# A SwiGLU feed-forward kernel: two weight slabs load behind two blocks of x, and two F tiles of the next tokens run by halves first

## The chip, the core and the metric

The kernel runs on one core of a Trainium2 chip. Its engines work side by side: TensorE (PE; its weight loads, PEld, overlap its products), VectorE (DVE), ScalarE (ACT), GpSimd (POOL) and SyncE (SP), which here only issues transfers. Sixteen DMA engines move the data. The metric is the time of one execution on the device in microseconds (us), the median over several runs.

## The reference

```
B, S, D, F = 1, 2048, 512, 1376          # all inputs bfloat16
g = silu(x @ w_gate)                     # x: S x D, w_gate: D x F
u = x @ w_up                             # w_up: D x F
out = (g * u) @ w_down                   # w_down: F x D
```

## The kernel before

**Tiles.** The 2048 tokens are cut into four blocks of 512 (c = 0 to 3), the 1376 columns of F into ten tiles of 128 (ft = 0 to 9) and a rest of 96, and D = 512 into four parts of 128. x is held transposed in `xT_sb`, the gate and up weights in `w_sb`, h = g * u in `h0_sb` (tokens 0-1023) and `h1_sb` (1024-2047). Products are collected in the eight banks of `psum`, each 512 numbers wide.

**Two ways to form a product.** A pair of F tiles (u) and a pair of token blocks (pi) make a unit, class `Unit`, which needs seven products of half the depth instead of eight, but sums of weights (`ss_sb`, made on POOL by `w_sums`) and differences of x blocks (`tt_sb`, made by `x_sums`, on DVE for tokens 0-1023) before them. Its products are L616 and L628. For tokens 0-1023 the units run for the pairs u = 2, 4, 3 alone. F tiles 0 to 3 of these tokens are done directly, product by product, at the start, while x and the weights still arrive: that is `gu_emit` (L424), with the helpers `gu_group` and `classic`. One group of L424 is one F tile, gate or up, for one token block: four depth parts by two column halves of the weight tile, 8 products of 512 columns. `gu_emit` can also do a part of the columns (n0 to n1). `classic_out` then puts silu of the gate bank into `sg_sb` (ACT, L332) and multiplies it with the up bank into h (DVE, L337), which frees the two banks.

**The start of the program.** Tokens 0-255 are loaded plainly into `xn_sb` and transposed on TensorE; the rest of x arrives through transposing transfers: `x0b` is tokens 256-511, `x1a` 512-767, `x1b` 768-1023, then `x2` and `x3` with 512 tokens each. The weights come in slabs of two F tiles, gate and up each by itself: `wg0`, `wu0` are F tiles 0 and 1, `wg2`, `wu2` tiles 2 and 3, `wg4`, `wu4` tiles 4 and 5, `wg8`, `wu8` tiles 8, 9 and the rest. All are issued by SP, in the order of the calls of `load`. TensorE's own order is: F tiles 0 and 1 of tokens 0-511 (x by halves of 256 columns for the gate), F tiles 2 and 3 of tokens 0-511 by `classic(0, [2, 3])`, then F tiles 0, 1 and 2 of tokens 512-1023, one tile after the other; then the rest columns (`plan_x` L488, `plan_y` L514), then the units and the down products (L726, L864, L876).

**What sets the order.** TensorE and SP run in the order of the calls. DVE, ACT and POOL take theirs from `Plan.schedule`, a list planner: of all operations that could run it takes the one with the earliest start by its own table of durations, then the one with the smaller priority number. For a transfer it uses a landing time: `load` adds each transfer's duration `lag` to a running sum `landed`, and a constant to that. So the constant and the order of the loads change the order that DVE, ACT and POOL get. Each engine then works strictly in this order and waits on semaphores: one count for each engine, and one semaphore for each transfer (30 for `wg0`, 21 `wu0`, 29 `wg2`, 20 `wu2`, 0 `x1a`, 1 `x1b`, 12 `wg4`, 28 `wu4`).

The first of the differences (`x_sums(0, "D", ...)`) reads both blocks of tokens 0-1023 and also waits for POOL's first sums of weights; POOL's next sums wait for the last of the differences.

Of the kernel before, what the change touches and what calls it, by code (L numbers as in the profile page):

```python
# [168 lines left out]
def bass_standalone__swiglu_ffn__prompt_kernel(nc, x, w_gate, w_up, w_down, out):  # L169
    _, S, D = x.shape  # L170
    F = w_gate.shape[1]
    P = 128
    KD = D // P
# [11 lines left out]
    HT = SC // 2  # L185
# [13 lines left out]
    with ExitStack() as es:  # L199
# [55 lines left out]
        def load(name, emit, writes, busy, lag):  # L255
            nonlocal landed
            landed += lag
            i = take(homes[name] if name in homes else rest[0])
            plan.add("S", emit, writes=writes, busy=busy, lag=1800, dma=(i, 16)).land = landed + (300 if landed < 10500 else 1600)

        slabs = [(0, 2), (2, 4), (4, 6), (6, 8), (8, NFF + 1)]
        slab_of = {ft: a for a, b in slabs for ft in range(a, b)}
# [10 lines left out]
        def load_slab(a, b):  # L273
            load_w(f"wg{a}", w_gate, 0, a * P, a * P, min(b * P, F))
            load_w(f"wu{a}", w_up, 1, a * P, a * P, min(b * P, F - 32))

        def load_x(name, t0, t1):
            load(
                name, lambda e: e.dma_start_transpose(xT_sb[:, :, t0:t1], xf[t0:t1, :]), [name], 1500, 4 * (t1 - t0)
            )  # L280
# [8 lines left out]
        load_w("wg0", w_gate, 0, 0, 0, slabs[0][1] * P)  # L289
        load_x("x0b", HT, SC)  # L290
        load_w("wu0", w_up, 1, 0, 0, slabs[0][1] * P)
        load_slab(*slabs[1])
        for i in range(2):
            load_x(f"x1{'ab'[i]}", SC + i * HT, SC + (i + 1) * HT)
        load_slab(*slabs[2])
        load_slab(*slabs[4])
        load_w("wut", w_up, 0, F, F - 32, F)
# [109 lines left out]
        def next_bank():  # L407
            nonlocal n_group
            b = turn[n_group % NB]
            n_group += 1  # L410
            return b
# [8 lines left out]
        def gu_emit(m, ft, c, b, dks, n0, n1):  # L420
            def emit(e):
                for dk in dks:
                    for h in (0, HC):
                        ins = e.matmul(  # L424
                            psum[h:h + HC, b, n0:n1], lhsT=w_sb[:, dk, m, ft * P + h:ft * P + h + HC],
                            rhs=xT_sb[:, dk, c * SC + n0:c * SC + n1], start=(dk == 0), stop=(dk == KD - 1),
                            tile_position=(0, h),
                        )
                return ins
            return emit  # L430
# [38 lines left out]
        def classic(c, fts, own=None):  # L469
            gates = [next_bank() for ft in fts] if own is None else own[:1]  # L470
            ups = [next_bank() for ft in fts] if own is None else own[1:]
            for ft, b in zip(fts, gates):
                gu_group(0, ft, c, b, own is not None)
            for ft, b in zip(fts, ups):
                gu_group(1, ft, c, b, own is not None)
            for ft, bg, bu in zip(fts, gates, ups):
                classic_out(ft, c, bg, bu)
# [67 lines left out]
        def w_sums(u, prio, after, casts, apart=False):  # L545

            f0, f1 = 2 * u * P, (2 * u + 1) * P
            slot = len(slot_of) % NSLOT
            slot_of[u] = slot
            at = lambda n: ss_sb[:, slot, W_SUM[n], :, :, :]  # L550
            wkeys = [[f"w{g}{slab_of[2 * u]}"] for g in "gu"]
            for ms in ((0, 1), (1, 2)) if apart else ((0, 2),):
                block = lambda k, f: w_sb[:, k * KH:(k + 1) * KH, ms[0]:ms[1], f:f + P].rearrange("p k m c -> p m k c")
                part = lambda n: at(n)[:, ms[0]:ms[1]]
                rd = lambda n: part(n).bitcast(FP32)
                keys = lambda n: [("ss", slot, n, m) for m in range(*ms)]
                reads = [k for m in range(*ms) for k in wkeys[m]]
                for n in ("S1", "S2", "S3", "S4"):
                    A11, A12, A21, A22 = (block(k, f) for f in (f0, f1) for k in range(2))
                    a, b, alu, of_ = {  # L560
                        "S1": (A21, A22, ALU.add, ()), "S2": (rd("S1"), A11, ALU.subtract, ["S1"]),
                        "S3": (A11, A21, ALU.subtract, ()), "S4": (A12, rd("S2"), ALU.subtract, ["S2"]),
                    }[n]
                    last = tt_op(
                        "G", part(n), a, b, alu, reads + [k for o in of_ for k in keys(o)], keys(n), prio,
                        620 if apart else 1180, after,
                    )
            for m in range(2):
                cast_op(
                    casts, at("A22")[:, m], w_sb[:, KH:2 * KH, m, f1:f1 + P], wkeys[m], [("ss", slot, "A22", m)], 8, 360,  # L570
                    after if casts == "G" else () if slot < 3 else [last],
                )
            return [last]
# [441 lines left out]
        units = [(pi, u) for pi in range(2) for u in U_ORDER[pi]]  # L1015
        early = [2 * u + i for u in range(NFF // 2) if u not in U_ORDER[0] for i in range(2)]
        sums = w_sums(0, 8, (), "A", True)
        classic(0, [2, 3])
        for ft in early[:3]:
            classic(1, [ft])  # L1020
        sums = x_sums(0, "D", 4, sums)
        for u in U_ORDER[0]:
            sums = w_sums(u, 2, sums, "A")
# [69 lines left out]
```

## Time and profile before

| | |
|---|---|
| Time, median of 3 runs | 115.72 us (115.47 to 116.23) |
| The profiled execution | 115.52 us |
| Its span on the core | 114.2 us |
| Granted TensorE clock | 1.00 |
| Moved by DMA | 9.84 MB, 22808 packets |
| SP's longest queue of loads | from 0.74 to 24.6 us |

All durations below are from this one profiled execution. Its time is 1.3 us longer than its span, and 0.2 us below the median of the three runs. The page groups work by line and engine; times in the chain and the timeline count from the start of the span. "PEld" rows are weight loads of TensorE: one waits on its own semaphore, and a product follows it. The busy time of PE is that of overlapping products, so rates are best read from a stretch: the length of a run of products over their count. TensorE starts cold, and its products before 5.35 us run at half of the later rate: six products of 512 columns take 2.72 us from 0.77 on.

### The profile page before, as it was taken

The page shows a single profiled execution, that of the slowest core. Times are in us where ns is not written, and L with a number is a line of the kernel's source. Part 1 is how long each engine was busy: PE and PEld are TensorE (multiplying, and loading weights), DVE is VectorE, ACT ScalarE, POOL GpSimd, SP SyncE. Part 2 cuts the span into 40 slices and gives each one's busy share as a digit, 9 for nine tenths or more (in the row PEclk, how much of TensorE's full clock was granted, in tenths as well). Part 3 has the DMA queues.
Part 4 walks back from the last instruction along what each step waited for, and adds up shares of the span by engine and source line. Part 5 has one row for each costly group of instructions (what it writes and reads, how often), then busy time and mean ns, then how long its engine had stood idle before and what let it go on. Part 6 is the DMA issues. An engine that isn't in the chain of part 4 may idle for free.

```text
span 114.2 us, 1765 instructions
## 1 busy us (share of the span) xinstructions
PE 110.7 (97%) x646; PEld 68.0 (60%) x654; DVE 76.5 (67%) x113; ACT 64.0 (56%) x123; POOL 62.2 (54%) x61
## 2 busy tenths in 40 slices
PE   7999999999999999999999999999999999999993
PEld 2665555456674858576776858653344557866452
DVE  0113799883956858493948668499999957486423
ACT  5344765866679895867678786740567960000000
POOL 1493004999999999999998999845000000000000
PEclk9999999999999999999999999999999999999999
DMA  3999999994000000000000000000031002227976
GB/s 101 235 276 237 321 190 225 271 361 101 0 0 0 3 0 3 0 0 6 0 3 0 0 0 0 0 0 0 17 127 46 0 0 46 46 52 183 201 200 197
DMA packets 22808, 9.84 MB, mean 86 GB/s; under 512 B 12848, under 2 KB 22672, under 8 KB 22800
## 3 DMA queue, kind: packets, MB, share of 16 engines
q1 hardware_dynamic: 20656, 8.69, 31.5%
q10 hardware_dynamic: 2144, 1.05, 3.2%
q8 instruction: 5, 0.08, 0.3%
q14 instruction: 3, 0.02, 0.1%
HBM read 4.75 MB, written 2.10 MB: 60 GB/s over the span
## 4 chain that ended last, share of the span: by engine, by line
PE 96%; DVE 1%; issue 1%
PE psum L616 32%; PE psum L726 15%; PE psum L628 12%; PE psum L424 11%; PE psum L864 10%; PE psum L876 4%; PE psum L488 3%; PE psum L754 3%; PE psum L350 2%; PE psum L435 2%; PE psum L514 2%; DVE o_sb L326 1%; PE psum L397 0%; PE psum L380 0%; PE psum L373 0%
## 5 line engine op out<-in xcount | busy, mean ns | idle before, releaser
L616 PE MATMUL psum<-tt_sb,ss_sb 128*128 128x512 f32 x160 | 40.0, 403 | 0.0
L616 PEld LDWEIGHTS psum<-tt_sb,ss_sb 128*128 128x128 f32 x160 | 29.7, 188 | 7.9 <-DVE ts_sb L337 0.6
L337 DVE TENSOR_TENSOR ts_sb<-r_sb,psum 128x512 f32<-128x512 f32 x32 | 20.6, 681 | 14.9 <-ACT r_sb L325 14.9
L337 POOL TENSOR_TENSOR h_sb<-sg_sb,ts_sb 128x512 bf16<-128x512 f32 x16 | 20.9, 1309 | 2.8 <-ACT sg_sb L332 2.8
L332 ACT ACTIVATE sg_sb<-psum 128x512 f32<-128x512 f32 x24 | 14.3, 599 | 11.2 <-PE psum L616 6.0
L325 ACT ACTIVATE r_sb<-psum 128x512 f32<-128x512 f32 x32 | 17.3, 594 | 4.5 <-PE psum L616 4.5
L337 DVE TENSOR_TENSOR h_sb<-sg_sb,psum 128x512 bf16<-128x512 f32 x24 | 16.3, 681 | 4.2 <-PE psum L424 3.9
L337 POOL TENSOR_TENSOR ss_sb<-w_sb 128x512 fp32r<-128x512 bf16 (+1 forms) x12 | 11.8, 997 | 12.6 <-DVE tt_sb L337 9.0
L726 PE MATMUL psum<-wd_sb,h_sb 128*128 128x512 bf16 (+2 forms) x98 | 17.9, 336 | 0.2 <-issue 0.2
L628 PE MATMUL psum<-xT_sb,w_sb 128*128 128x512 bf16 x59 | 14.2, 380 | 0.4 <-issue 0.2
L726 PEld LDWEIGHTS psum<-wd_sb,h_sb 128*128 128x128 bf16 x100 | 8.3, 98 | 9.2 <-issue 1.0
L424 PE MATMUL psum<-xT_sb,w_sb 128*64 128x512 bf16 (+1 forms) x128 | 12.8, 359 | 0.0
L332 ACT ACTIVATE sg_sb<-ts_sb 128x512 f32<-128x512 f32 x16 | 10.1, 634 | 1.6 <-DVE ts_sb L337 1.6
L424 PEld LDWEIGHTS psum<-xT_sb,w_sb 128*64 128x64 bf16 x128 | 7.3, 114 | 5.4 <-DMA w_sb<-in_w_up_dram 0.3
L628 PEld LDWEIGHTS psum<-xT_sb,w_sb 128*128 128x128 bf16 x64 | 5.5, 98 | 8.0 <-issue 2.5
L326 DVE COPY psum<-psum 128x512 f32<-128x512 f32 x8 | 5.6, 699 | 1.2 <-PE psum L616 0.5
L337 POOL TENSOR_TENSOR ss_sb<-w_sb,ss_sb 128x512 fp32r<-128x512 bf16 (+1 forms) x6 | 6.0, 1007 | 0.3
L337 POOL TENSOR_TENSOR ss_sb<-ss_sb,w_sb 128x512 fp32r<-128x512 f32 (+1 forms) x6 | 6.0, 1000 | 0.0
L326 DVE CAST o_sb<-psum 128x512 bf16<-128x512 f32 (+2 forms) x6 | 3.0, 512 | 4.2 <-PE psum L726 3.1
L337 POOL TENSOR_TENSOR ss_sb<-wd_sb 128x640 fp32r<-128x640 bf16 x4 | 5.6, 1406 | 0.0
L864 PE MATMUL psum<-tt_sb,ss_sb 128*128 128x512 f32 x20 | 5.6, 417 | 0.0
L864 PE MATMUL psum<-th_sb,ss_sb 128*128 128x512 f32 x20 | 5.5, 411 | 0.0
(72 smaller groups left out, 121.4 us busy)
## 6 DMA issues: line engine op xcount, KB each, us to landing
wd_sb<-in_w_down_dram SPq DMA_DIRECT2D x1, 1280.0 KB, 8.5
w_sb<-in_w_gate_dram SPq DMA_DIRECT2D x4, 256.0 KB, 4.0
w_sb<-in_w_up_dram SPq DMA_DIRECT2D x4, 256.0 KB, 4.2
out_dram<-o_sb SPq DMA_DIRECT2D x7, 128.0 KB, 1.8
out_dram<-xT_sb ACTq DMA_DIRECT2D x4, 128.0 KB, 2.5
out_dram<-xT_sb ACTq DMA_DIRECT2D x2, 256.0 KB, 3.2
w_sb<-in_w_gate_dram SPq DMA_DIRECT2D x1, 352.0 KB, 5.2
w_sb<-in_w_up_dram SPq DMA_DIRECT2D x1, 320.0 KB, 5.6
```

The source lines that it names most:

```text
L325: return e.activation(out, src, ACT.Copy)
L326: return e.tensor_copy(out, src)
L332: "A", lambda e: e.activation(out, src, ACT.Silu), reads, writes, busy, A_LAG, prio
L337: engs, lambda e: e.tensor_tensor(out, a, b, alu), reads, writes, busy,
L424: ins = e.matmul(psum[h:h + HC, b, n0:n1], lhsT=w_sb[:, dk, m, ft * P + h:ft * P + h + HC], rhs=xT_sb[:, dk, c * SC + n0:c * SC + n1], sta ...
L488: ins = e.matmul(psum[m:m + HC, b, :], lhsT=w_sb[:, dk, 0, XC0 + m:XC0 + m + HC], rhs=xT_sb[:, dk, c * SC:(c + 1) * SC], start=(dk == 0), ...
L616: ins = e.matmul(bank(dst), lhsT=s[:, k, :], rhs=t[:, k, :], start=(start and k == 0), stop=(k == KH - 1), skip_group_check=True,)
L628: ins = e.matmul(bank(dst), lhsT=w_sb[:, k0 + k, m, f:f + P], rhs=xT_sb[:, k0 + k, c:c + SC], start=(start and k == 0), stop=(k == KH - 1) ...
L726: ins = e.matmul(psum[:, b, 0:c1 - c0], lhsT=hrows(F_ORDER[n], t, 0, P), rhs=wd_sb[:, F_ORDER[n], c0:c1], start=(start and n == n0), stop= ...
L754: ins = e.matmul(bank(b), lhsT=lhsT, rhs=rhs, start=(start and n == 0), stop=(n == 2 and (kind == "T" or not start)), tile_position=(r0, 0 ...
L864: ins = e.matmul(bank(dst), lhsT=self.ds[s][:, j, self.q, :], rhs=self.dt[t][:, j, :], start=(start and n == 0), stop=(n == NFF // 2 - 1), ...
L876: ins = e.matmul(bank(dst), lhsT=wd_sb[:, 2 * j + a, d * P:(d + 1) * P], rhs=h0_sb[:, 2 * j + a, 0:SC], start=(n == 0), stop=(n == NFF // ...
```

## The change

Three things are edited. In `load`, the landing time that the planner uses for a transfer is the running sum plus 500 ns throughout, where it was plus 300 below 10500 and plus 1600 from there on. In the order of loads, `x1a` and `x1b` are issued right behind `wu0`, and `wg2`, `wu2` behind them. In TensorE's order, F tiles 0 and 1 of tokens 512-1023 run before F tiles 2 and 3 of tokens 0-511. Their four groups (gate and up of two tiles, four banks) run twice over: first all four for tokens 512-767, which need `x1a` alone, then all four for tokens 768-1023, which need `x1b`. F tile 2 of tokens 512-1023 follows `classic(0, [2, 3])` as before. What is computed stays the same.

```diff
@@ -256,7 +256,7 @@
             landed += lag
             i = take(homes[name] if name in homes else rest[0])
-            plan.add("S", emit, writes=writes, busy=busy, lag=1800, dma=(i, 16)).land = landed + (300 if landed < 10500 else 1600)
+            plan.add("S", emit, writes=writes, busy=busy, lag=1800, dma=(i, 16)).land = landed + 500
@@ -289,9 +289,9 @@
         load_w("wu0", w_up, 1, 0, 0, slabs[0][1] * P)
-        load_slab(*slabs[1])
         for i in range(2):
             load_x(f"x1{'ab'[i]}", SC + i * HT, SC + (i + 1) * HT)
+        load_slab(*slabs[1])
         load_slab(*slabs[2])
@@ -1015,9 +1015,15 @@
         sums = w_sums(0, 8, (), "A", True)
+        pairs = [(ft, m, next_bank()) for ft in early[:2] for m in range(2)]
+        for h in range(2):
+            for ft, m, b in pairs:
+                emit = gu_emit(m, ft, 1, b, range(KD), h * HT, (h + 1) * HT)
+                pe(emit, [f"x1{'ab'[h]}", f"w{'gu'[m]}{slab_of[ft]}"], [("b", b)], KD / 2)
+        for (ft, m, g), (_, _, u) in zip(pairs[::2], pairs[1::2]):
+            classic_out(ft, 1, g, u)
         classic(0, [2, 3])
-        for ft in early[:3]:
-            classic(1, [ft])
+        classic(1, early[2:3])
         sums = x_sums(0, "D", 4, sums)
```

Here `early` is [0, 1, 2, 3], so `early[2:3]` is F tile 2. Lines behind L1017 move down by 6; all lines that the prediction names lie ahead of it. The numbers of `psum` banks move too: the four groups by halves take banks 4 (gate 0), 5 (up 0), 6 (gate 1) and 7 (up 1), F tiles 2 and 3 of tokens 0-511 take 0 to 3, and F tile 2 of tokens 512-1023 takes 4 and 5.

SP's queue, near its start: in the difference, what stands with a minus left its place and what stands with a plus came there.

```order
 L279 DMA_TRANSPOSE xT_sb<-in_x_dram 128x4x256
 L267 DMA w_sb<-in_w_up_dram 128x4x256
+L279 DMA_TRANSPOSE xT_sb<-in_x_dram 128x4x256 x2
 L267 DMA w_sb<-in_w_gate_dram 128x4x256
 L267 DMA w_sb<-in_w_up_dram 128x4x256
-L279 DMA_TRANSPOSE xT_sb<-in_x_dram 128x4x256 x2
 L267 DMA w_sb<-in_w_gate_dram 128x4x256
 L267 DMA w_sb<-in_w_up_dram 128x4x256
```

The first two rows are `x0b` and `wu0`; `x1a` and `x1b` pass `wg2` and `wu2`, and the rest keeps its place.

TensorE before, from the first product that needs `wg2` on (L424; s_dma29 is `wg2`, s_dma20 `wu2`, s_dma0 `x1a`, s_dma1 `x1b`, s_A and s_D the counts of ACT and DVE):

```order
L424 MATMUL psum<-xT_sb,w_sb 64x512 [waits s_dma29]
L424 MATMUL psum<-xT_sb,w_sb 64x512 x15
L424 MATMUL psum<-xT_sb,w_sb 64x512 [waits s_dma20]
L424 MATMUL psum<-xT_sb,w_sb 64x512 x15
L424 MATMUL psum<-xT_sb,w_sb 64x512 [waits s_dma1,s_dma0,s_A]
L424 MATMUL psum<-xT_sb,w_sb 64x512 x7
L424 MATMUL psum<-xT_sb,w_sb 64x512 [waits s_D]
L424 MATMUL psum<-xT_sb,w_sb 64x512 x7
```

And TensorE at the same place now:

```order
L424 MATMUL psum<-xT_sb,w_sb 64x256 [waits s_dma0]
L424 MATMUL psum<-xT_sb,w_sb 64x256 x31
L424 MATMUL psum<-xT_sb,w_sb 64x256 [waits s_dma1]
L424 MATMUL psum<-xT_sb,w_sb 64x256 x31
L424 MATMUL psum<-xT_sb,w_sb 64x512 [waits s_dma29,s_A]
L424 MATMUL psum<-xT_sb,w_sb 64x512 x7
L424 MATMUL psum<-xT_sb,w_sb 64x512 [waits s_D]
L424 MATMUL psum<-xT_sb,w_sb 64x512 x7
L424 MATMUL psum<-xT_sb,w_sb 64x512 [waits s_dma20,s_A]
```

The wait for both blocks of x, which stood behind 32 products of F tiles 2 and 3, is now two waits, each ahead of 32 products of 256 columns; the slabs of F tiles 2 and 3 are wanted behind these.

DVE before, from the first of the x differences (tt0_sb) on; the sg_sb number tells the products of h apart:

```order
L337 TENSOR_TENSOR tt0_sb<-xT_sb 128x1024 [waits s_dma1,s_G,s_dma0]
L337 TENSOR_TENSOR h0_sb<-sg_sb2,psum 128x512 [waits s_P,s_A]
L337 TENSOR_TENSOR tt0_sb<-xT_sb,tt0_sb 128x1024 [waits s_D]
L337 TENSOR_TENSOR h0_sb<-sg_sb3,psum 128x512 [waits s_P,s_A]
L337 TENSOR_TENSOR tt0_sb<-xT_sb 128x1024 [waits s_D]
L337 TENSOR_TENSOR h0_sb<-sg_sb4,psum 128x512 [waits s_A,s_P]
L337 TENSOR_TENSOR tt0_sb<-xT_sb,tt0_sb 128x1024 [waits s_D]
L337 TENSOR_TENSOR h0_sb<-sg_sb5,psum 128x512 [waits s_P,s_A]
L337 TENSOR_TENSOR h0_sb<-sg_sb0,psum 128x512 [waits s_A,s_P]
```

And DVE at the same place now:

```order
L337 TENSOR_TENSOR tt0_sb<-xT_sb 128x1024 [waits s_G,s_dma1,s_dma0]
L337 TENSOR_TENSOR tt0_sb<-xT_sb,tt0_sb 128x1024 [waits s_D]
L337 TENSOR_TENSOR h0_sb<-sg_sb2,psum 128x512 [waits s_A,s_P]
L337 TENSOR_TENSOR tt0_sb<-xT_sb 128x1024 [waits s_D]
L337 TENSOR_TENSOR h0_sb<-sg_sb3,psum 128x512 [waits s_A,s_P]
L337 TENSOR_TENSOR tt0_sb<-xT_sb,tt0_sb 128x1024 [waits s_D]
L337 TENSOR_TENSOR h0_sb<-sg_sb4,psum 128x512 [waits s_P,s_A]
L337 TENSOR_TENSOR h0_sb<-sg_sb5,psum 128x512 [waits s_P,s_A]
L337 TENSOR_TENSOR h0_sb<-sg_sb0,psum 128x512 [waits s_P,s_A]
```

The second difference moved ahead of the first product of h, and the last difference ahead of the third; sg_sb2 and sg_sb3 now belong to F tiles 0 and 1 of tokens 512-1023, sg_sb4 and sg_sb5 to F tiles 2 and 3 of tokens 0-511.

## The prediction

> **What bounds the kernel now.** I read the page's busy time and chain first, because they say which engine an edit has to shorten.
>
> ```profile
> PE 110.7 (97%) x646; PEld 68.0 (60%) x654; DVE 76.5 (67%) x113; ACT 64.0 (56%) x123; POOL 62.2 (54%) x61
> PE 96%; DVE 1%; issue 1%
> ```
>
> TensorE is busy for 97% of the span, and 96% of the chain that ended last is its own work. The chain in order of time (start, length, what) shows how tight it is around the change.
>
> ```profile
> 4.92 2.02 PE psum L424 x32
> 6.94 0.03 issue
> 6.97 10.55 PE psum L424 x96
> 17.52 1.73 PE psum L488 x16
> 19.25 0.86 PE psum L514 x8
> 20.11 1.73 PE psum L488 x16
> ```
>
> The 96 products of L424 that the change reorders run from 6.97 to 17.52 with nothing between them: 10.55 / 96 = 0.110 us each, 1.76 us for a group of 16. The next stages follow at once. So the loads of this stage hide completely today. The third view is the list of waits (engine and tile, who was waited for, total us, times, longest); I looked for the weight loads, PEld, that waited for something other than TensorE.
>
> ```profile
> PEld psum L616 <- DVE ts_sb L337: 0.6, 2, 0.3
> PEld psum L424 <- DMA w_sb<-in_w_up_dram: 0.3, 1, 0.3
> PEld psum L616 <- DVE h_sb L337: 0.3, 1, 0.3
> PEld psum L488 <- DVE h_sb L337: 0.2, 1, 0.2
> ```
>
> The only load that TensorE waited for here is the up weights of F tiles 0 and 1, which the change leaves in their place. The three DVE rows add up to 1.1 us on PEld, and part of that lies under running products. A better order has no more than this to collect.
>
> **The change part by part.** *The products.* Of the 96 products, 16 stay, 32 of 512 columns become 64 of 256, and 48 of 512 follow. The price of a 256-column product is in the stretch where x 256-511 is consumed today: its weight loads, one to a product, run back to back.
>
> ```profile
> 5.58 1.09 PEld L424 LDWEIGHTS psum<-xT_sb,w_sb 128*64 128x64 bf16 x20
> ```
>
> That is 0.0545 us each; 64 of them take 3.49 us against 32 x 0.110 = 3.52 us before. The split costs -0.03, that is nothing.
>
> *When TensorE asks for each load now.* The 16 up products of F tiles 0 and 1 end at 6.97 + 1.76 = 8.73. There it now wants x 512-767; 32 x 0.0545 = 1.74 us later, at 10.47, x 768-1023; at 12.22 the gate slab of F tiles 2 and 3; 16 products later, at 13.98, its up slab. All 96 end at 6.97 + 1.76 + 3.49 + 48 x 0.110 = 17.50, as before.
>
> *When the loads land now.* These are SP's issues (start, length), and then the times from issue to landing, in the order x 256-511, up 0-1, gate 2-3, up 2-3, x 512-767, x 768-1023, gate 4-5, up 4-5.
>
> ```profile
> 1.67 1.33 SPq L279 DMA_TRANSPOSE xT_sb<-in_x_dram  x1
> 3.05 0.57 SPq L267 DMA_DIRECT2D w_sb<-in_w_up_dram  x1
> 3.66 0.51 SPq L267 DMA_DIRECT2D w_sb<-in_w_gate_dram  x1
> 4.21 0.51 SPq L267 DMA_DIRECT2D w_sb<-in_w_up_dram  x1
> 4.76 2.15 SPq L279 DMA_TRANSPOSE xT_sb<-in_x_dram  x1
> 6.95 1.51 SPq L279 DMA_TRANSPOSE xT_sb<-in_x_dram  x1
> 8.50 0.58 SPq L267 DMA_DIRECT2D w_sb<-in_w_gate_dram  x1
> 9.13 0.51 SPq L267 DMA_DIRECT2D w_sb<-in_w_up_dram  x1
> ...
> xT_sb<-in_x_dram SPq DMA_TRANSPOSE x1, 3.6
> w_sb<-in_w_up_dram SPq DMA_DIRECT2D x1, 256.0 KB, 3.9
> w_sb<-in_w_gate_dram SPq DMA_DIRECT2D x1, 256.0 KB, 4.1
> w_sb<-in_w_up_dram SPq DMA_DIRECT2D x1, 256.0 KB, 4.4
> xT_sb<-in_x_dram SPq DMA_TRANSPOSE x1, 4.8
> xT_sb<-in_x_dram SPq DMA_TRANSPOSE x1, 5.0
> w_sb<-in_w_gate_dram SPq DMA_DIRECT2D x1, 256.0 KB, 4.3
> w_sb<-in_w_up_dram SPq DMA_DIRECT2D x1, 256.0 KB, 4.5
> ```
>
> Sums: 5.27, 6.95, 7.76, 8.61, 9.56, 11.95, 12.80 and 13.63. From 6.95 to 9.56 three loads of 256 KB land 0.81 to 0.95 apart whatever their kind, although they were issued long before: the queue is worked off in order and its bytes set the pace. Moving two slabs of 0.81 + 0.85 = 1.66 us behind the two x loads therefore brings x 512-767 from 9.56 to 7.90 and x 768-1023 from 11.95 to at most 10.29.
>
> A second limit is SP. A transposed load keeps SP 1.33 to 2.15 us, and landed 5.27 - 3.00 = 2.27 and 9.56 - 6.91 = 2.65 us after its issue ended. Issued at 3.66, x 512-767 lands between 3.66 + 1.33 + 2.27 = 7.26 and 3.66 + 2.15 + 2.65 = 8.46, all before 8.73. I take 7.9. No row shows a transposed load right behind one slab only, so both ends stay.
>
> The second x load is odd: it landed 2.39 us after the first, not 0.9. Two windows of 0.2 us, from 9.8 and from 10.0, show why (packets, and the fetch queue with its share of 16 engines; the last row is the page's for the whole span).
>
> ```profile
> DMA packets 104, 0.04 MB, mean 212 GB/s; under 512 B 75, under 2 KB 103, under 8 KB 103
> q8 instruction: 1, 0.02, 33.6%
> ...
> DMA packets 20, 0.01 MB, mean 51 GB/s; under 512 B 0, under 2 KB 20, under 8 KB 20
> q8 instruction: 5, 0.08, 0.3%
> ```
>
> Packets under 512 B are the transposed ones; the last of them start before 10.0. The x load was off the other engines by then, but one instruction fetch of 0.08 / 5 MB = 16 KB held one engine for 0.336 x 16 x 0.2 = 1.08 us, and the load behind it on that engine landed last. Five fetches fit TensorE's 646 + 654 instructions, 260 to a fetch. The Trainium skill, "Runtime: NRT & Kernel Launch", section Instruction fetch mechanics, says the same of their size and calls the cost of crossing a block "mostly hidden". The trace differs: here it is the difference between a landing near 10.5 (9.56 + 0.95) and one at 11.95. By that rule the second x load would land at 7.9 + 0.9 = 8.8 and no fetch could hold TensorE.
>
> With or without the fetch: without, 7.90 + 0.95 = 8.85; with it as before, 10.29. If SP is slow too, 3.66 + 2 x 2.15 = 7.96 ends the issue, and 11.95 - 8.46 = 3.49 is the delay with the fetch: 11.45. Against 10.47 the wait is between nothing and 0.98 us. I take nothing, since both landings on the queue's own pace lie before 10.47.
>
> The slabs that moved back: the gate slab now lands where the old follower of the x loads did, less the two: 12.80 - 1.66 = 11.14, wanted at 12.22; the up slab 13.63 - 1.66 = 11.97, wanted at 13.98. Cover 1.1 and 2.0 us; without it the wait would be that much less. From gate 4-5 on, the same bytes stand ahead as before.
>
> *The queues behind.* Before, the first difference of x (DVE, tt_sb) waits for x 768-1023, and the halves of F tiles 2 and 3 follow it.
>
> ```profile
> 12.12 1.23 DVE L337 TENSOR_TENSOR tt_sb<-xT_sb 128x1024 fp32r<-128x1024 bf16 x1 [2.43 <-DMA xT_sb<-in_x_dram]
> 18.46 1.27 DVE L337 TENSOR_TENSOR h_sb<-sg_sb,psum 128x512 bf16<-128x512 f32 x2
> 9.01 0.68 POOL L337 TENSOR_TENSOR ss_sb<-w_sb,ss_sb 128x256 fp32r<-128x256 bf16 x1
> 18.69 2.27 POOL L337 TENSOR_TENSOR ss_sb<-w_sb 128x512 fp32r<-128x512 bf16 x2 [9.01 <-DVE tt_sb L337]
> ```
>
> Now two differences stand ahead of the first product of tokens 512-1023 (bank 5) and three ahead of the second (bank 7); TensorE wants bank 5 again at 17.50 - 0.88 = 16.6. From a start t that product ends at t + 2 x 1.23 + 0.68 = t + 3.14, so t may be as late as 13.4; t is the later of 9.7 (POOL's first sums end) and the landing, 10.3. Cover 3 us. POOL then starts its sums some 1.8 us before 18.69. Its order changes behind that: two x differences pass one product of h, whose ts_sb DVE overwrites next.
>
> ```profile
> 34.05 1.28 POOL L337 TENSOR_TENSOR h_sb<-sg_sb,ts_sb 128x512 bf16<-128x512 f32 x1
> 38.37 0.67 DVE L337 TENSOR_TENSOR ts_sb<-r_sb,psum 128x512 f32<-128x512 f32 x1
> ```
>
> The product ends at 35.33 today and is wanted at 38.37. Two sums of 2.27 us together pass it, 1.8 us of head start stand against them: 35.8. Cover 2.6 us, so nothing.
>
> Sum: 115.52 us for the profiled execution, -0.03 for the pieces, 0 for the loads, 0 for the queues: 115.5. The median of the three runs, 115.72, lies 0.2 above that execution; I forecast 115.6.
>
> **The rivals.** *A late second half of x (slower).* TensorE stops inside the new group, at 10.47, for x 768-1023. For it: the fetch falls near the same instruction, and the new pieces reach it sooner; against it: the queue's pace alone gives 10.29. It decides from a landing of 10.47 and costs up to 0.98: 115.7 to 116.6.
>
> *The x loads land no earlier.* If something other than the queue's order set 9.56 and 11.95, TensorE would stop 0.83 at 8.73 and, 1.74 after that, from 11.30 to 11.95: 115.6 + 0.83 + 0.65 = 117.1. The steady 0.81 to 0.95 speaks against it.
>
> *The earlier sums pay off (faster).* DVE and POOL run 1.8 us ahead, and the three DVE waits shrink. All of them give 1.1: 114.5; half of them on TensorE itself, 115.0. Against it: two of the three lie in units whose DVE work waits for products, not for sums.
>
> **How the numbers follow.** No change to speak of 0.68; late second half 0.15; no earlier landing 0.06; pay-off 0.11. Range: pay-off by half less a little for spread, 114.9, to the full price of the late half, 116.6; outside lie the full pay-off and most of 117.1. Runs of this kernel before spread over 0.76 us, so about 1% (1.16 us) is what a measurement tells from no change. Faster by over that: a third of the pay-off and 0.02 of spread, 0.06. Slower: all of the no-landing case, a third of the late half and 0.02 of spread, 0.13. Within: 0.81.
>
> **What would show it.** Right: the chain has 16 + 64 + 48 products of L424 with no issue piece longer than 0.1 us, ending near 17.5; the two x loads land near 7.9 and 8.8 to 10.3; DVE's first tt_sb starts near 10; PEld has no wait for xT_sb. Wrong: a PEld wait for in_x_dram or for in_w_gate_dram of more than 0.3 us, L488 starting after 18.0, or TensorE gaps after 22 us that were not there before.

## The result, and the profile after

The changed kernel took 115.28 us (114.73 to 115.63, 18 runs) beside 115.61 us (115.24 to 116.23, 18 runs) for the kernel before: ratio 0.9966, 95% interval 0.9952 to 0.998. A second series gave 115.61 beside 115.71 us: ratio 0.9996, 0.9981 to 1.001. The two intervals do not touch, so one series alone tells less than its interval says; together they put the change between nothing and 0.4 us faster, with 0.2 in the middle. The forecast was 115.6 us and no change within 1%. All ratios compare undisturbed executions; the one that was profiled for `cast_behind` took 190.87 us and is not read. What follows asks where the small rest comes from, and why it is not larger.

The profiled execution of the changed kernel took 114.90 us, with a span of 113.6 and a clock of 1.00: 0.62 us less than the profiled execution before. First its page, busy time and shares of the chain:

```profile
PE 110.6 (97%) x686; PEld 69.3 (61%) x686; DVE 76.8 (68%) x113; ACT 63.7 (56%) x123; POOL 62.4 (55%) x61
PE 92%; DMA 3%; SPq 2%; DVE 1%; issue 0%
```

TensorE is as full as before. That 5% of the chain are now DMA and SP is no new cost: the chain now starts with the load that TensorE waited for at the head. Its pieces in order of time:

```profile
3.05 3.54 DMA w_sb<-in_w_up_dram
6.59 0.04 issue
6.63 10.59 PE psum L424 x128
17.22 1.73 PE psum L488 x16
18.95 0.86 PE psum L514 x8
19.81 1.74 PE psum L488 x16
```

The up products of F tiles 0 and 1 start at 6.63 instead of 6.97; that is 0.34 of the 0.62 us. The 16 + 64 + 48 products run without a stop, 10.59 us against 10.55. TensorE's waits for something other than itself:

```profile
PEld psum L424 <- DMA w_sb<-in_w_up_dram: 0.5, 1, 0.5
...
PEld psum L488 <- DMA xT_sb<-in_x_dram: 0.3, 1, 0.3
...
PEld psum L616 <- DVE h_sb L337: 0.3, 1, 0.3
```

There is none for x in L424, and one that is new, for the last block of x in the rest columns (L488). The row `DVE ts_sb`, 0.6 us before, is gone. This is where the other 0.28 us lie, in the units. The chain there, before and then after:

```profile
34.66 1.67 PE psum L628 x7
36.34 4.77 PE psum L616 x20
41.11 1.74 PE psum L628 x8
42.85 4.63 PE psum L616 x20
```

```profile
34.31 1.74 PE psum L628 x8
36.05 4.56 PE psum L616 x20
40.61 1.74 PE psum L628 x8
42.35 4.56 PE psum L616 x20
```

Twenty products of L616 took 4.77 and 4.63 us where they now take 4.56 both times: 0.28 us. The timeline of the other engines just ahead of it, before (start, length, engine, what, count, idle time ahead of it and who ended it):

```profile
32.92 1.17 POOL L337 TENSOR_TENSOR ss_sb<-w_sb,ss_sb 128x512 fp32r<-128x512 bf16 x1
...
34.13 0.72 ACT L541 ACTIVATE ss_sb<-w_sb 128x256 fp32r<-128x256 bf16 x2 [0.60 <-POOL ss_sb L337]
34.76 1.06 ACT L325 ACTIVATE r_sb<-psum 128x512 f32<-128x512 f32 x2
...
35.37 1.28 DVE L337 TENSOR_TENSOR ts_sb<-r_sb,psum 128x512 f32<-128x512 f32 x2 [2.42 <-ACT r_sb L325]
```

Read from the bottom: TensorE waited for DVE's ts_sb; DVE waited 2.42 us for ACT's copy of a product (r_sb); that copy stood on ACT's queue behind two copies of weights (L541), and these waited 0.60 us for POOL's fourth sum of the third unit's weights. After:

```profile
31.05 1.17 POOL L337 TENSOR_TENSOR ss_sb<-w_sb,ss_sb 128x512 fp32r<-128x512 bf16 x1
...
33.13 0.73 ACT L541 ACTIVATE ss_sb<-w_sb 128x256 fp32r<-128x256 bf16 x2
33.89 1.09 ACT L325 ACTIVATE r_sb<-psum 128x512 f32<-128x512 f32 x2
...
34.52 1.29 DVE L337 TENSOR_TENSOR ts_sb<-r_sb,psum 128x512 f32<-128x512 f32 x2 [1.86 <-ACT r_sb L325]
```

POOL is 1.87 us earlier, and ACT does not wait. The cause is far ahead, in the same view:

```profile
9.83 1.23 DVE L337 TENSOR_TENSOR tt_sb<-xT_sb 128x1024 fp32r<-128x1024 bf16 x1 [0.48 <-POOL ss_sb L337]
...
16.49 2.28 POOL L337 TENSOR_TENSOR ss_sb<-w_sb 128x512 fp32r<-128x512 bf16 x2 [6.79 <-DVE tt_sb L337]
```

x 768-1023 landed at 8.54, not 11.95, so DVE's first difference starts at 9.83 instead of 12.12 and POOL's sums start at 16.49 instead of 18.69.

### The profile page after: what moved, and what is told of

It is laid out like the page before. It is cut to its first block, busy times and chain, and to the rows that moved or that the text cites. A ratio compares the mean times of both kernels' runs of the same rounds, so it can differ in the third digit from the quotient of the medians.

```text
span 113.6 us, 1838 instructions
## 1 busy us (share of the span) xinstructions
PE 110.6 (97%) x686; PEld 69.3 (61%) x686; DVE 76.8 (68%) x113; ACT 63.7 (56%) x123; POOL 62.4 (55%) x61
## 4 chain that ended last, share of the span: by engine, by line
PE 92%; DMA 3%; SPq 2%; DVE 1%; issue 0%
PE psum L616 32%; PE psum L726 15%; PE psum L628 12%; PE psum L864 10%; PE psum L424 9%; PE psum L876 4%; DMA w_sb<-in_w_up_dram 3%; PE psum L488 3%; PE psum L754 3%; PE psum L514 2%; PE psum L435 2%; SPq L279 1%; DVE o_sb L326 1%; SPq L267 0%; SPq L284 0%
## 5 line engine op out<-in xcount | busy, mean ns | idle before, releaser
L616 PE MATMUL psum<-tt_sb,ss_sb 128*128 128x512 f32 x160 | 39.8, 402 | 0.0
L616 PEld LDWEIGHTS psum<-tt_sb,ss_sb 128*128 128x128 f32 x160 | 30.0, 188 | 7.3 <-DVE h_sb L337 0.3
L726 PE MATMUL psum<-wd_sb,h_sb 128*128 128x512 bf16 (+2 forms) x100 | 18.4, 337 | 0.0
L628 PE MATMUL psum<-xT_sb,w_sb 128*128 128x512 bf16 x64 | 15.4, 381 | 0.0
L726 PEld LDWEIGHTS psum<-wd_sb,h_sb 128*128 128x128 bf16 x100 | 8.3, 98 | 9.2 <-issue 1.0
L424 PE MATMUL psum<-xT_sb,w_sb 128*64 128x256 bf16 (+1 forms) x160 | 12.6, 316 | 0.2 <-DMA w_sb<-in_w_up_dram 0.2
L424 PEld LDWEIGHTS psum<-xT_sb,w_sb 128*64 128x64 bf16 x160 | 8.7, 110 | 4.0 <-DMA w_sb<-in_w_up_dram 0.5
L628 PEld LDWEIGHTS psum<-xT_sb,w_sb 128*128 128x128 bf16 x64 | 5.5, 98 | 7.9 <-issue 2.5
```

Source lines behind the costliest of these rows:

```text
L424: ins = e.matmul(psum[h:h + HC, b, n0:n1], lhsT=w_sb[:, dk, m, ft * P + h:ft * P + h + HC], rhs=xT_sb[:, dk, c * SC + n0:c * SC + n1], sta ...
L616: ins = e.matmul(bank(dst), lhsT=s[:, k, :], rhs=t[:, k, :], start=(start and k == 0), stop=(k == KH - 1), skip_group_check=True,)
L628: ins = e.matmul(bank(dst), lhsT=w_sb[:, k0 + k, m, f:f + P], rhs=xT_sb[:, k0 + k, c:c + SC], start=(start and k == 0), stop=(k == KH - 1) ...
L726: ins = e.matmul(psum[:, b, 0:c1 - c0], lhsT=hrows(F_ORDER[n], t, 0, P), rhs=wd_sb[:, F_ORDER[n], c0:c1], start=(start and n == n0), stop= ...
```

## The experiments

Three theories stood at the start. **A**: the gain is at the head, because x behind the up weights lets these land sooner (6.59 against 6.93). **B**: the gain is in the units, through POOL's earlier sums, as just read. The rival to both: what is left is scatter, and the change as such moves nothing. For each kernel but `cast_behind` the table gives the ratio to the kernel before with its interval, the start of the up products (the head), and three stretches between first products in the timeline: direct products (up products to L488), rest columns (L488 to L628), units (L628 to L726). The lead is how long before the first product of L628 POOL starts its unit sums. The last column adds the three stretches.

| kernel | ratio (interval) | head | direct | rest | units | lead | sum |
|---|---|---|---|---|---|---|---|
| before | 1 | 6.97 | 10.38 | 5.29 | 52.63 | 3.95 | 68.30 |
| changed | 0.9966 (0.9952-0.998) | 6.63 | 10.43 | 5.29 | 52.34 | 5.86 | 68.06 |
| after_again | 0.9996 (0.9981-1.001) | 7.00 | 10.43 | 5.28 | 52.33 | 6.02 | 68.04 |
| const_only | 0.9995 (0.9972-1.0018) | 7.27 | 10.39 | 5.28 | 52.49 | 4.08 | 68.16 |
| loads_only | 1.0135 (1.0104-1.0165) | 7.03 | 12.36 | 5.27 | 52.39 | 7.33 | 70.02 |
| products_only | 1.0049 (1.0032-1.0066) | 7.42 | 11.25 | 5.29 | 52.30 | 6.84 | 68.84 |
| slab_between | 0.9988 (0.9972-1.0005) | 7.11 | 10.40 | 5.29 | 52.30 | 6.37 | 67.99 |
| whole | 0.9988 (0.997-1.0006) | 7.44 | 10.36 | 5.43 | 52.35 | 6.67 | 68.14 |
| pool_held | 0.9965 (0.9943-0.9987) | 7.38 | 10.42 | 5.81 | 52.30 | 4.76 | 68.53 |
| pool_held_more | 1.0079 (1.0058-1.01) | 7.08 | 10.42 | 5.50 | 53.43 | 3.04 | 69.35 |
| pool_free_before | 1.0077 (1.0053-1.01) | 7.54 | 10.36 | 6.52 | 52.35 | 10.39 | 69.23 |
| cast_behind_2 | 0.9998 (0.9977-1.0019) | 7.55 | 10.38 | 5.28 | 52.42 | 4.05 | 68.08 |
| gate_early | 1.0037 (1.0021-1.0054) | 6.74 | 10.42 | 6.14 | 52.33 | 6.53 | 68.89 |

(In the trace of before one record of the first L628 products is missing; its start is taken one product, 0.22 us, ahead.) From L726 to TensorE's last product no stretch differs by more than 0.05 us between kernels; behind that product the span of `loads_only` lasts 0.4 us longer than the others.

### The two halves of the change, each alone

`const_only` is the kernel before with the new landing constant, which alone changes the order of DVE, ACT and POOL a little.

```diff
-            plan.add("S", emit, ...).land = landed + (300 if landed < 10500 else 1600)
+            plan.add("S", emit, ...).land = landed + 500
```

> The kernel before with the planner's landing constant alone (plus 500 throughout). Only ACT's order among four weight copies near 13 to 17 us differs. Theory A (the x blocks behind the up slab let that slab land earlier) and theory B (POOL's sums start earlier, so ACT no longer waits for the fourth sum of the third pair): no change, ratio 0.999 to 1.001; the up slab lands near 6.9, ACT waits some 0.6 us for POOL near 34 us. Rival (the constant itself gives a better order): near 0.9966.

Measured 0.9995 (0.9972 to 1.0018). The first series' gain lies outside that interval, a gain of 0.2 us does not. In the profile the lead is nearly as short as before, and the wait of ACT for POOL is still there:

```profile
34.30 0.72 ACT L541 ACTIVATE ss_sb<-w_sb 128x256 fp32r<-128x256 bf16 x2 [0.47 <-POOL ss_sb L337]
```

`loads_only` adds the new order of loads to that and leaves TensorE's order as it was.

```diff
-        load_slab(*slabs[1])
         for i in range(2):
             load_x(f"x1{'ab'[i]}", SC + i * HT, SC + (i + 1) * HT)
+        load_slab(*slabs[1])
```

> The kernel before with the constant and the new order of the loads, TensorE's order as before. TensorE then wants the gate slab of F tiles 2 and 3 at 8.4, which lands near 9.9: a stop of 1.5 us. Theory A: the up slab lands near 6.6 as in the changed kernel, so 0.3 is won ahead of the stop; with theory B 0.25 more behind it: 115.6 + 1.5 - 0.3 - 0.25 = 116.5. Rival (the up slab's landing is chance): it may land anywhere from 6.6 to 6.95, about 116.8.

Measured 1.0135 (1.0104 to 1.0165), 117.20 us, more than the 116.5 to 116.8 that were expected: the stop is about 2 us, not 1.5. The up slab landed at 6.99, not near 6.6 as theory A had it. TensorE wants the gate slab of F tiles 2 and 3 right behind the up products, and the slab lands at 10.69; the row of the waits:

```profile
PEld psum L424 <- DMA w_sb<-in_w_gate_dram: 2.3, 1, 2.3
```

`products_only` is the reverse: TensorE's new order, with the loads and the constant of before.

```diff
+        for h in range(2):
+            for ft, m, b in pairs:
...
-        for ft in early[:3]:
-            classic(1, [ft])
+        classic(1, early[2:3])
```

> The changed order of TensorE with the old order of the loads and the old constant. Theories A and B and the prediction: TensorE stops for x 512-767 from 8.73 to 9.56 and for x 768-1023 from 11.30 to 10.5 (no stop) or to 12.0 (with the instruction fetch in its way): 0.83 to 1.5 us, 116.4 to 117.1. The up slab lands near 6.9 by theory A, since a slab follows it. Rival (the new order of the products wins by itself): below 115.9.

Measured 1.0049 (1.0032 to 1.0066), 116.27 us, just under the 116.4 to 117.1 that were expected. TensorE waits for x 512-767, 1.12 us on its weight loads, and the stretch is 0.87 us longer than before:

```profile
9.97 2.11 PEld L424 LDWEIGHTS psum<-xT_sb,w_sb 128*64 128x64 bf16 x40 [1.12 <-DMA xT_sb<-in_x_dram]
```

In this execution x 768-1023 landed 0.93 us behind x 512-767 (10.86 and 9.93), in the old order of loads; the fetch of instructions came at 12.97, behind both. The pair of landings 0.9 apart that the prediction derived for a run without a fetch is seen here. So neither half pays alone: each by itself makes TensorE stop, although with each the units shrink as in the changed kernel (52.39 and 52.30), and only together do they leave the direct products as they were.

### Are the halves needed, and must both slabs stand behind x?

`whole` is the changed kernel with each of the four groups in one piece of 512 columns.

```diff
-        for h in range(2):
-            for ft, m, b in pairs:
-                emit = gu_emit(m, ft, 1, b, range(KD), h * HT, (h + 1) * HT)
-                pe(emit, [f"x1{'ab'[h]}", f"w{'gu'[m]}{slab_of[ft]}"], [("b", b)], KD / 2)
+        for ft, m, b in pairs:
+            gu_group(m, ft, 1, b)
```

> The changed kernel with F tiles 0 and 1 of tokens 512-1023 in products of 512 columns, not by halves: TensorE wants both x blocks at 8.4 to 8.7, and the second lands near 8.5 when the instruction fetch is not in its way. Prediction's costing: the halves cost nothing and gain only what the second block is late: no change against the changed kernel in most runs (0.9966), up to 0.2 us more; if the fetch hits the second block, 1.0 to 1.5 us more, near 1.008.

Measured 0.9988 (0.997 to 1.0006). No stop in the direct products, 10.36 us for them: x 768-1023 landed at 8.84 and is wanted at 7.44 + 1.76 = 9.20. The halves cost 0.07 us (10.43 less 10.36) and move the time by which x 768-1023 is needed back by 1.74 us. In this execution they were not needed; with a fetch ahead of that landing, as in the profile of before, they would be by the prediction's 10.29. No run showed that case.

`slab_between` is the changed kernel with `wg2` ahead of the two x loads and `wu2` behind them.

```diff
+        load_w("wg2", w_gate, 0, 2 * P, 2 * P, 4 * P)
         for i in range(2):
             load_x(f"x1{'ab'[i]}", SC + i * HT, SC + (i + 1) * HT)
-        load_slab(*slabs[1])
+        load_w("wu2", w_up, 1, 2 * P, 2 * P, 4 * P)
```

> The changed kernel with the gate slab of F tiles 2 and 3 back between the up slab of tiles 0, 1 and the two x blocks. TensorE wants x 512-767 at 8.7 and it lands near 8.5, x 768-1023 at 10.5 and it lands near 9.5: no stop. Theory A: the up slab lands near 6.9 again, and 0.3 us of the gain goes: ratio to the kernel before 0.999, the part of theory B (0.2) aside. Rival (that landing is chance): it may land at 6.6 too, and the ratio stays near 0.9966.

Measured 0.9988 (0.9972 to 1.0005), x 512-767 at 8.73: the weight loads waited 0.23 us for it, the products did not stop. The up slab landed at 7.01, as theory A expected for a slab behind it, but that lies within the scatter shown next. It does as well as the changed kernel within what can be told.

### The head

`after_again` is the changed kernel once more, on the chip of the last series.

> The changed kernel as it is, a second look on the same chip as the three beside it. Both theories expect the ratio that it had, 0.995 to 0.998. What the look adds is whether the small things in its first profile return: no wait of ScalarE for GpSimd's sums near 33 us, the units' stretch (first product of L628 to first of L726) at 52.3 us, and a wait of 0.3 us for x in the rest columns. Theory A (the gain is the head of the program) expects the up products of F tiles 0 and 1 to start near 6.6 again; the rival takes that for chance and expects any value between 6.6 and 7.5.

Measured 0.9996 (0.9981 to 1.001), outside the 0.995 to 0.998 that both theories expected. The chain of its profile:

```profile
7.00 10.59 PE psum L424 x128
17.59 1.73 PE psum L488 x16
```

The up products start at 7.00, not 6.63. Over all profiles with x behind the up weights the start lies between 6.63 and 7.44, and over those with a slab behind them between 6.97 and 7.55. So 0.37 us lie between two profiles of one kernel, more than A was to explain, and A is not borne out. It is not excluded as a smaller effect: the means of the two kinds, seven profiles and six, are 7.04 and 7.31, with a scatter of 0.24 to 0.3 in each. The landing of the up slab itself, which is what A is about, has means of 6.93 and 7.15. It does not always set the head: in `whole` and `pool_free_before` the slab was there at 6.91 and 6.83, and TensorE came to it only at 7.44 and 7.54, because its products ran at half their later rate until 6.35 and 6.6 us (5.35 in the kernel before). The rest of this second profile repeats the first to 0.02 us: units 52.33, no wait of ACT for POOL.

### The lead of POOL's sums

`pool_held` is the changed kernel with one more wait: POOL's first unit sum also waits for DVE's h of F tile 2, tokens 512-1023.

```diff
+        held, by = plan.writer["ss", slot_of[2], "S1", 0], plan.writer["h", early[2], 1]
...
         plan.schedule()
+        held.deps.add(by)
+        held.raw.add(by)
```

> The changed kernel; POOL's first sum for a unit waits also for DVE's product of F tile 2 of tokens 512-1023, so POOL starts these sums near 18.2 instead of 16.5, nearly as in the kernel before (18.7). Loads, products and all orders stay. Theory B: ACT waits for POOL near 33.5 again, 0.4 to 0.8 us, and the time rises by 0.15 to 0.25 us: ratio to the kernel before 0.998 to 0.999. Rival (theory A is all): stays at 0.9966.

Measured 0.9965 (0.9943 to 0.9987), and no wait of ACT in the profile. POOL did start at 18.85, as late as before by the clock, but the first product of L628 came 0.97 us later than in the kernel before, partly by the head and partly by a wait for x (below). So the lead was 4.76 us, more than the 3.95 of before. The experiment had not reached the point where the theories part; it told nothing against B, and nothing for it.

`pool_held_more` holds the same sum until DVE's last difference of the rest columns.

```diff
+        held, by = plan.writer["ss", slot_of[2], "S1", 0], plan.writer["htx", 0]
...
         plan.schedule()
+        held.deps.add(by)
+        held.raw.add(by)
```

(`htx` 0 is DVE's first product of the rest columns; the expectation calls it a difference.)

> The changed kernel with GpSimd's sums for the first unit held until VectorE has made the last difference of the rest columns (about 19.5 us). GpSimd then leads the units' first product by about 3.0 us, less than in the kernel before (3.95). Theory B (below a lead of about 4.3 us each microsecond is one of waiting, through ScalarE's copy behind the late sum): ScalarE waits 1.2 to 1.5 us for GpSimd near 34 us, the units' stretch grows to 53.3 to 53.7, ratio 1.005 to 1.009. The rival (the lead has nothing to do with the gain): ratio 0.9965 as in the changed kernel.

Measured 1.0079 (1.0058 to 1.01), 1.0 us slower than the changed kernel beside it. POOL started at 19.96, the lead was 3.04, and the wait is back, in the timeline and on TensorE's weight loads:

```profile
35.32 0.72 ACT L541 ACTIVATE ss_sb<-w_sb 128x256 fp32r<-128x256 bf16 x2 [1.44 <-POOL ss_sb L337]
...
37.30 0.30 PEld L616 LDWEIGHTS psum<-tt_sb,ss_sb 128*128 128x128 f32 x2 [1.13 <-DVE ts_sb L337]
37.90 1.24 PEld L616 LDWEIGHTS psum<-tt_sb,ss_sb 128*128 128x128 f32 x6 [0.30 <-DVE ts_sb L337]
```

The units grow to 53.43 us, 1.09 more than in the changed kernel. The three profiles that show the wait lie on a line: lead 3.95, wait 0.60; lead 4.08, wait 0.47; lead 3.04, wait 1.44. Lead and wait add up to 4.5 or 4.55 each time, and at leads of 4.76 and more there is no wait. TensorE loses about 0.33 less in the units than ACT waits: 0.29, 0.15 and 1.09 us. Theory B holds, with a size of 0.29 us in these profiles.

`cast_behind` and `cast_behind_2` are one kernel in two series: the kernel before with the two weight copies behind the two copies of products that they held up.

```diff
         plan.schedule()
+        acts = plan.order["A"]
+        i = acts.index(late[0])
+        acts[i:i + 4] = acts[i + 2:i + 4] + late
```

> The kernel before; on ACT the two weight copies of the third pair, which wait for POOL's fourth sum (0.60 us at 34.13), stand behind the next two copies of psum banks into r_sb instead of ahead of them. Nothing else moves. Theory B: DVE's ts_sb at 35.37 comes some 1.0 us earlier, the two waits of TensorE's weight loads for ts_sb near 36 us go, and 0.2 to 0.28 us is won: ratio 0.998. Rival (these waits lie under running products): no change, 1.000.

> The kernel before with ScalarE's two weight copies for pair 3 behind its next two copies of products (r_sb), a second look for a clean profile. Theory B (ScalarE's wait for GpSimd's fourth sum holds up the copies behind it): the wait stays or moves with the weight copies, but the r_sb copies start 0.6 us earlier against the products, PEld has no wait for ts_sb, the units' stretch falls from 52.6 to 52.3, ratio 0.997 to 0.999. The rival (that wait costs nothing): stretch 52.6, ratio 1.000.

Measured 0.998 (0.9961 to 0.9998) and 0.9998 (0.9977 to 1.0019). From the profile of the second:

```profile
34.71 1.09 ACT L325 ACTIVATE r_sb<-psum 128x512 f32<-128x512 f32 x2 [0.63 <-PE psum L616]
35.34 1.28 DVE L337 TENSOR_TENSOR ts_sb<-r_sb,psum 128x512 f32<-128x512 f32 x2 [1.83 <-ACT r_sb L325]
35.69 0.72 ACT L541 ACTIVATE ss_sb<-w_sb 128x256 fp32r<-128x256 bf16 x2
```

The lead is still short, 4.05, but ACT now waits for the product itself, and the weight copies behind it find their sum ready. From the first product of L628, DVE's ts_sb starts 12.13 us on (35.34 less 23.21); before it was 12.73, in the changed kernel 12.17. PEld has no wait for ts_sb, and the units take 52.42. Two copies moved in ACT's order give, in the profile, 0.21 of the 0.29 us that the changed kernel gains there; by time alone the two series do not settle an effect of this size.

`pool_free_before` gives the kernel before a long lead in another way: POOL's unit sums no longer wait for DVE's differences.

```diff
-        for u in U_ORDER[0]:
-            sums = w_sums(u, 2, sums, "A")
+        for n, u in enumerate(U_ORDER[0]):
+            sums = w_sums(u, 2, sums if n else first, "A")
```

> The kernel before; POOL's sums for the units follow its first sums at once instead of DVE's differences of x, so they start when the slab of F tiles 4 and 5 is there, near 13.7 instead of 18.7. The planner moves the copies on ACT too. Theory B: ACT no longer waits for POOL near 34 us, 0.2 to 0.28 us won, ratio 0.998. Against it could stand that DVE and POOL now work side by side from 13.7 to 18.5, where POOL idled: if they slow each other by more than a few per cent the gain shrinks. Rival: 1.000.

Measured 1.0077 (1.0053 to 1.01), slower, where both theories expected no loss. The units are at 52.35 as B says, but the rest columns took 6.52 us instead of 5.29. DVE and POOL now work side by side:

```profile
13.69 0.68 DVE L337 TENSOR_TENSOR h_sb<-sg_sb,psum 128x512 bf16<-128x512 f32 x1
14.02 3.25 POOL L337 TENSOR_TENSOR ss_sb<-w_sb 128x512 fp32r<-128x512 bf16 x2 [4.09 <-DMA w_sb<-in_w_up_dram]
14.29 1.96 DVE L337 TENSOR_TENSOR tt_sb<-xT_sb,tt_sb 128x1024 fp32r<-128x1024 bf16 x1
16.18 0.67 DVE L337 TENSOR_TENSOR h_sb<-sg_sb,psum 128x512 bf16<-128x512 f32 x1
16.77 1.57 DVE L337 TENSOR_TENSOR tt_sb<-xT_sb 128x1024 fp32r<-128x1024 bf16 x1
...
21.70 1.44 PEld L488 LDWEIGHTS psum<-xT_sb,w_sb 128*64 128x64 bf16 x16 [1.53 <-DVE h_sb L337]
```

The differences take 1.96, 1.57 and 1.58 us instead of 1.22, POOL's first two sums 3.25 instead of 2.27, and the product of h with one operand from psum still 0.67. The three add 0.74 + 0.35 + 0.36 = 1.45 us to DVE's queue, and TensorE's weight loads then wait 1.53 for an h behind it. The Trainium skill, "SBUF — State Buffer", section Who interferes with whom, says that a DVE instruction with two inputs in SBUF contends with a GpSimd instruction that reads SBUF, and one with a single input there does not. These rows agree.

### The new wait for the last block of x

`gate_early` is the changed kernel with the gate products of F tile 3, tokens 512-1023, moved from behind the rest columns to their middle, so that `x2` and `x3` are wanted 0.86 us later.

```diff
         y_out(0, 4)
+        gu_group(0, early[3], 1, 6)
         plan_x(2, 5)
...
-        classic(1, early[3:], [6, 7])
+        gu_group(1, early[3], 1, 7, True)
+        classic_out(early[3], 1, 6, 7)
```

> The changed kernel with the gate products of F tile 3 of tokens 512-1023 ahead of the rest columns of x 1024-2047, so that x2 and x3 are wanted 8 x 0.11 = 0.9 us later. If the late landing of x3 costs time in ordinary runs, as 0.3 us of wait in the first profile of the changed kernel says, this one is 0.2 to 0.4 us faster than the changed kernel: ratio 0.993 to 0.995. The rival: what TensorE waits there it no longer waits at the next place that needs other engines, and the ratio stays at 0.9965.

Measured 1.0037 (1.0021 to 1.0054): slower by half a microsecond than the changed kernel beside it. The rest columns less the moved group take 6.14 - 0.86 = 5.28 us, which is what they took in that kernel too, so its profile held no stop that could be saved; and the units, which now hold 0.86 us less work, take as long as ever. In DVE's queue the last product of h stands behind four others; the timelines of the two, first of `gate_early`:

```profile
26.54 0.69 DVE L337 TENSOR_TENSOR h_sb<-sg_sb,psum 128x512 bf16<-128x512 f32 x1
...
27.28 1.66 PE L616 MATMUL psum<-tt_sb,ss_sb 128*128 128x512 f32 x6 [0.69 <-DVE h_sb L337]
```

And of `after_again`:

```profile
25.94 0.69 DVE L337 TENSOR_TENSOR h_sb<-sg_sb,psum 128x512 bf16<-128x512 f32 x1
```

That product starts 3.24 and 3.23 us behind the first product of L628 (26.54 less 23.30, 25.94 less 22.71). In the changed kernel the gate group of F tile 3 stood in between as cover; moved away, TensorE arrives early and stands. Neither expectation had this. By the stretches the kernel should lose 0.85 us to `after_again`; the medians differ by 0.57. Whether the rest is a stop for x that it avoids in other executions was not shown.

The wait for x itself is real, and changes from one execution to the next. In the profiles of the changed kernel and of `pool_held`, whose loads are the same:

```profile
20.50 0.57 PEld L488 LDWEIGHTS psum<-xT_sb,w_sb 128*64 128x64 bf16 x8 [0.30 <-DMA xT_sb<-in_x_dram]
```

```profile
21.76 0.57 PEld L488 LDWEIGHTS psum<-xT_sb,w_sb 128*64 128x64 bf16 x8 [0.82 <-DMA xT_sb<-in_x_dram]
```

`x3` landed at 20.45 and at 21.72 us; in `after_again`, the first of these kernels once more, at 20.67 and without this wait. At 20.45 the products behind were still covered (rest columns 5.29 as before), at 21.72 the wait cost 0.52 us, in `pool_held_more` 0.21 and in `whole` 0.14. The landing goes with the first instruction fetch: in the four profiles where that starts between 9.86 and 10.34 us, all with the old order of loads, `x3` landed between 19.81 and 20.12, and none has this wait; in the nine where it starts at 10.63 or later, `x3` landed between 20.45 and 21.72. One of these nine, `products_only` (20.93; it has no wait, since it is late as a whole), has the old order of loads, so it is not shown that the order of loads moves `x3`. The time of `pool_held` (0.9965) suggests that such a stop is not in most of its executions: with it the stretches add up to a ratio of 1.002.

## Why the prediction was right, point by point

**The sum.** 115.5 for the profile stood against 114.90 and 115.26, 115.6 for the median against 115.28 and 115.61 in the two series. "No change to speak of" was right, and the range held both medians. That the second median meets the forecast to 0.01 us is luck: the same kernel gave 0.33 less in the first series.

**The pieces.** -0.03 was forecast for 64 half products. Direct products grew by 0.05 us (10.43 against 10.38), and without the halves they take 10.36. So the halves cost 0.05 to 0.07 where they were to win 0.03: a small term, as forecast, with the other sign.

**The loads.** x 512-767 was put at 7.9 between 7.26 and 8.46, and landed at 7.58 and 7.99 in the two profiles of the changed kernel; x 768-1023 at 8.85 without a fetch or 10.29 with one, and landed at 8.54 and 8.99. For the 8.54, its issue in the timeline and the time to its landing in the list of issues:

```profile
4.95 1.49 SPq L279 DMA_TRANSPOSE xT_sb<-in_x_dram  x1
...
xT_sb<-in_x_dram SPq DMA_TRANSPOSE x1, 3.6
```

The fetch came at 10.72 us and lasted 0.96, when x was in. Whether it strikes x or a slab was left open in the prediction, and that was fair: over the profiles it starts anywhere from 9.86 to 14.43. The slabs of F tiles 2 and 3 were put at 11.14 and 11.97 and landed at 9.94 and 11.11, in the second profile at 10.85 and 11.68. The two landings from which they were taken had the fetch ahead of them; that this is why they came out late is a reading.

One step here failed: "From gate 4-5 on, the same bytes stand ahead as before." The bytes do, but the landings moved: that of `x3` by 0.6 us in the first profile and by 0.9 in the second. One sign named for being right, no wait of PEld for xT_sb, therefore did not come: in L488 it waited 0.30 us, as much as the prediction still allowed. SP's queue, before and after:

```profile
10.22 1.66 SPq L267 DMA_DIRECT2D w_sb<-in_w_up_dram  x2
11.93 5.73 SPq L279 DMA_TRANSPOSE xT_sb<-in_x_dram  x2
```

```profile
9.30 3.11 SPq L267 DMA_DIRECT2D w_sb<-in_w_up_dram  x2
12.46 5.82 SPq L279 DMA_TRANSPOSE xT_sb<-in_x_dram  x2
```

SP reaches the two loads earlier and is held in them longer; then it writes the two transposed loads for 5.8 us, and `x3` lands behind that (20.45 less 18.28, 19.81 less 17.66: 2.2 us each). In the changed kernel the sixteen DMA engines move 20 GB/s from 15.0 to 16.0 us and 289 from 16.4 to 17.0. So before the bulk of `x2` moves they wait for SP and not SP for them, and `x3` comes behind it; what was cover before is gone.

What held SP was not tried by itself, but it goes with the instruction fetch. In nine profiles the fetch ends before SP is done with the slab loads, and SP comes free of them 0.7 to 1.5 us after that end. In the four others (`loads_only`, `products_only`, `slab_between`, `whole`) the fetch begins only after SP is free, and there the two transposed loads took 6.7 to 7.4 us instead of 5.0 to 6.0.

**The queues behind.** The cover of 3 us for DVE and of 2.6 for POOL held, and POOL did start about 2 us earlier. "So nothing" is the term that was mis-sized: it is -0.2 to -0.3 us. The argument against the pay-off, "two of the three lie in units whose DVE work waits for products, not for sums", stopped one step short. DVE waits for ACT's copy of a product, and the copy stood in ACT's queue behind one that waited for POOL's sum. The pay-off that was priced at up to 1.1 us is this one wait, 0.6 us on ACT and 0.3 on TensorE. Of the other two rows, that of h_sb on L616 did not change, and that of h_sb on L488 (0.2) went without effect: the rest columns take 5.29 us in both.

**The rivals.** No stop for x 768-1023 appeared in any profile with both halves of the change. "The x loads land no earlier" is refuted by the landings; what it would have looked like stands in `products_only`, with 0.9 us of stop.

**The sum by stretches.** The table's last column leaves the head out. Its difference to the kernel before, over 115.6 us, gives 0.998 for the changed kernel, 1.015 for `loads_only`, 1.005 for `products_only`, 1.009 for `pool_held_more`, 1.008 for `pool_free_before`, 1.005 for `gate_early`; measured were 0.9966 and 0.9996, 1.0135, 1.0049, 1.0079, 1.0077 and 1.0037. All others but `pool_held` agree within 0.002 too. So the change is worth about 0.2 us: 0.29 gained in the units, 0.05 lost in the pieces, and now and then a stop for `x3` on top. The part of the first series beyond that (0.9966) is not explained by any of these; the head, by chance or by A, is large enough for it, but that it did this was not shown and stays open.

## What to carry to other kernels

Follow a wait to its end, through each engine's queue: the row names the instruction that was waited for, and the one that holds it up stands ahead of it on that engine and may wait for a third. If two loads trade places, their consumers have to trade too: either half of this change alone was slower, by 0.5 and 1.4%. Ask how much slack an early producer needs (here a lead of 4.5 us) before a further gain is expected of making it earlier, and what covers a step before it is moved away.

## What was not expected of the hardware

- One instruction fetch of about 1 us on one of the sixteen DMA engines goes with a delay of a whole transfer by more than that: in the four profiles where the fetch starts between 9.86 and 10.34 us, x 768-1023 landed 2.4 to 2.5 us behind x 512-767, and in the nine where it starts later 0.9 to 1.3 us behind it.
- The head scatters: SP issued the first four loads of all these kernels at the same times to 0.02 us, the last of them landed anywhere from 6.59 to 7.51 us, and the up products that need it started from 6.63 to 7.55 us, a spread three times the gain studied here. In two of these profiles it was not the load that set the start but the time for which TensorE's products still ran at half their later rate.
- DVE and POOL side by side slow each other: a difference of x on DVE went from 1.22 to as much as 1.96 us, a sum of weights on POOL from 1.16 to as much as 2.14, both with all inputs in SBUF.
